# The first tile of rows loaded in two halves from two queues, and three issues reordered, in a two-layer attention and MLP kernel

## The chip, the cores and the metric

The kernel runs on one core of a Trainium2 chip. The metric is the device time of one execution in microseconds; lower is better. Times of single instructions come from one profiled execution.

## The reference

The input is a sequence of 2048 rows of 576 features in bfloat16. Four residual stages are applied, A, B, A, B:

```
x = x + A(layernorm(x));  x = x + B(layernorm(x));  and the same once more
A: q, k, v = x @ wqkv, 32 heads of 18
   phi(t) = where(t > 0, t + 1, exp(t)) + 1e-6
   kv = sum over rows of phi(k) v;  z = sum over rows of phi(k)
   o = phi(q) kv / (phi(q) z + 1e-6);  return o @ wo
B: y = layernorm(x);  h = gelu(y @ w1 + b1)   (576 -> 4608)
   return h @ w2 + b2                         (4608 -> 576)
```

## The kernel before

All weights and all rows stay in SBUF (on-chip memory). The rows are 16 tiles of 128 (`x_sb[:, t, :]`). For a tile, VectorE (DVE in the profile) computes the layer norm's statistics in two halves of 288 columns (`ln_st`, then `ln_mv`), GpSimd (POOL) the reciprocal standard deviation (`ln_rstd`), and VectorE the normalised rows (`y_ring`). TensorE (PE) transposes them into PSUM (`tp`), ScalarE (ACT) copies them to `yT`, and TensorE multiplies with the key and value weights `wkv_sb` into `k_ps`. ScalarE takes the exponential (`phi_e`), VectorE forms phi(k) (`pk`), and TensorE sums its products with the rows (`side_ps`, `rk_ps`).

Of the first weights, `wkv_sb`, there are five blocks of 128 input features; the fifth has 64 rows. A product for a half of the keys goes over the five blocks in order, so the last 64 rows are used last. `load_wkv(a, b, to)` asks for columns a to b: one DMA for the four whole blocks, one for the last 64 rows. The first half of the keys needs columns 0 to 288; the second product needs columns 288 to 576 and 72 value columns besides.

The order on every engine is written out by hand: each engine's wrapper (`vec`, `act`, `pool`, `sp`) chains every instruction to the one before it. DMAs are issued by SyncE (`sp`) or ScalarE (`act`) and stand in program order with that engine's other instructions; an instruction that waits for a semaphore holds all behind it on the same engine. In the trace the DMAs take eight completion semaphores in turn, and a DMA that reuses one is not issued before the earlier transfer with it has landed.

The kernel begins with lines 367 to 378: two tiles of rows and the first half of the key weights on SyncE, a dummy Exp on ScalarE (`act_dummy`, which brings the table of the exponential into ScalarE; it reads `neg_half`, written by GpSimd), the third tile on ScalarE, the second half of the key weights on SyncE, the 72 value columns on ScalarE, and three more tiles on SyncE. Meanwhile VectorE clears buffers, and TensorE runs ten products on zeros (`warm_ps`). Then come the first tile's statistics, `norms[0]`, the statistics of the second tile, the first tile's normalised rows in two pieces, its transposes, and so on: VectorE has the statistics of the first four tiles in front of the first `pk`.

Of the kernel before, what the change touches and what calls it, by code (L numbers as in the profile page):

```python
# [7 lines left out]
ACT = mybir.ActivationFunctionType  # L8
# [6 lines left out]
S, D, F, H, DH = 2048, 576, 4608, 32, 18  # L15
P = 128
# [14 lines left out]
HALF = D // 2  # L31
# [4 lines left out]
def build(tc, A_x, A_wqkv, A_wo, B_w1, B_b1, B_w2, B_b2, out, n_layers=4):  # L36
    nc = tc.nc
    with ExitStack() as ctx:
# [23 lines left out]
        vec, act = InOrder(nc.vector, "VectorE"), InOrder(nc.scalar, "ScalarE")  # L62
        pool, sp = InOrder(nc.gpsimd, "GpSimd"), InOrder(nc.sync, "SyncE")

        x_in = A_x.flatten_outer_dims()
# [32 lines left out]
        neg_half = const.tile([P, 1], F32, name="neg_half")  # L98
# [88 lines left out]
        wkv_sb = const.tile([P, KD, 2 * D], BF16, name="wkv_sb")  # L187
# [6 lines left out]
        x_sb = const.tile([P, NT, D], BF16, name="x_sb")  # L194
# [21 lines left out]
        act_dummy = const.tile([P, 1], F32, name="act_dummy")  # L216
# [104 lines left out]
        def load_x(t, by=sp):  # L321
            by.dma_start(out=x_sb[:, t, :], in_=x_in[t * P:(t + 1) * P, :])

        def load_wkv(a, b, to, by=sp):
            src, dst = slice(D + a, D + b), slice(to, to + b - a)
            by.dma_start(out=wkv_sb[:, 0:4, dst],
                         in_=A_wqkv[0:4 * P, src].rearrange("(k p) n -> p k n", p=P))
            by.dma_start(out=wkv_sb[0:64, 4, dst], in_=A_wqkv[4 * P:D, src])
# [36 lines left out]
            vec.tensor_copy(out=b1T[:], in_=tp[:, 0:NF])  # L365

        FIRST_X = 6
        load_x(0)
        load_x(1)
        load_wkv(0, HALF, 0)  # L370
        act.activation(out=act_dummy[:, 0:1], in_=neg_half[:, 0:1], func=ACT.Exp)
        load_x(2, act)
        load_wkv(HALF, D, HALF)
        load_wkv(D + V4, 2 * D, D, act)
        load_x(3)
        tc.add_manual_dep(sp.last_inst.ins, act.last, NOSYNC, reason="loads' order")
        load_x(4)
# [1071 lines left out]
@with_exitstack  # L1449
def kernel(  # L1450
    ctx: ExitStack,
    tc: tile.TileContext,
    A_x: bass.AP,
    A_wqkv: bass.AP,
    A_wo: bass.AP,
    B_x: bass.AP,
    B_w1: bass.AP,
    B_b1: bass.AP,
    B_w2: bass.AP,
    B_b2: bass.AP,  # L1460
    out: bass.AP,
):
    build(tc, A_x, A_wqkv, A_wo, B_w1, B_b1, B_w2, B_b2, out)
# [30 lines left out]
```

## Time and profile before

| what | value |
|---|---|
| median of 3 runs | 740.86 us (740.81 to 740.91) |
| profiled execution, time | 740.7 us |
| its span, first to last instruction | 738.8 us |
| TensorE busy | 733.3 us, 99% of the span |
| VectorE busy | 272.4 us, 37% |
| ScalarE busy | 300.8 us, 41% |
| granted TensorE clock | 1.0 throughout |
| DMA share, first 12.2 us | 0.76 |
| DMA share, after 60 us | 0.14 |

The share of an engine is busy time over the span; a wait on an engine costs time only where the chain that ends last goes through it. The time of an execution holds 1.9 us around the span. In rows of the timelines the first number is the start in microseconds from the span's start, the second the duration; an engine's name with a "q" is its sequencer, which issues DMAs; "x2" joins two instructions. Behind the row, in brackets, stands the idle time before it and what ended it.

### The profile page before, as it was taken

What the parts mean: (1) busy time and instruction counts of PE and PEld (TensorE: products, weight loads), DVE (VectorE), ACT (ScalarE), POOL (GpSimd) and SP (SyncE); (2) the same over time, 40 slices, a digit from 0 to 9 for tenths busy, and PEclk for the clock granted to TensorE, in tenths of its full rate; (3) what the DMA queues carried; (4) which work ended last, traced back from release to release, by engine and by line L of the source; (5) the groups of instructions that cost most, each with busy time, mean ns of one, the idle gap of its engine ahead of it and who ended that gap; (6) DMA issues with size and microseconds to landing.
All of it is one profiled execution on the core that took longest, in us unless ns stands there. A gap on an engine that the chain in (4) does not pass through costs nothing.

```text
span 738.8 us, 21166 instructions
## 1 busy us (share of the span) xinstructions
PE 733.3 (99%) x9142; PEld 578.4 (78%) x9151; DVE 272.4 (37%) x693; ACT 300.8 (41%) x667; POOL 131.9 (18%) x414
## 2 busy tenths in 40 slices
PE   8999999999999999999999999999999999999998
PEld 4666758996798679768987676789768976996695
DVE  8868744534224403300376594551410060000000
ACT  5776733007601740374035666220373047106700
POOL 4541000422121202200223120031300130010010
PEclk9999999999999999999999999999999999999999
DMA  8955220112200220110023001202020002000000
GB/s 203 245 172 182 76 76 29 26 31 52 36 11 26 37 38 18 31 24 2 18 77 94 24 6 31 74 2 55 17 37 2 18 19 35 10 18 10 1 18 17
DMA packets 61315, 35.02 MB, mean 47 GB/s; under 512 B 37126, under 2 KB 61222, under 8 KB 61222
## 3 DMA queue, kind: packets, MB, share of 16 engines
q1 hardware_dynamic: 60390, 33.43, 17.8%
q8 instruction: 71, 1.16, 0.7%
q10 hardware_dynamic: 832, 0.25, 0.2%
q14 instruction: 22, 0.18, 0.1%
HBM read 21.70 MB, written 4.93 MB: 36 GB/s over the span
## 4 chain that ended last, share of the span: by engine, by line
PE 98%; DVE 1%; DMA 0%; issue 0%; POOL 0%; DVEq 0%
PE m_ps L227 38%; PE hp_ps L227 20%; PE h_ps L227 18%; PE k_ps L227 5%; PE q_ps L227 5%; PE wo_ps L227 5%; PE rk_ps L227 4%; PE side_ps L227 1%; PE tp L476 0%; DVE ln_st L53 0%; PE den_ps L227 0%; PE kvwo_ps L227 0%; PE kv_ps L227 0%; DMA x_sb<-in_A_x_dram 0%; PE rden_ps L227 0%; DVE pk L53 0%
## 5 line engine op out<-in xcount | busy, mean ns | idle before, releaser
L227 PEld LDWEIGHTS <-units 64*128 64x128 bf16 (+1 forms) x5070 | 320.5, 94 | 12.9 <-issue 0.2
L227 PE MATMUL m_ps<-w_sb,units 64*128 64x288 bf16 (+2 forms) x4432 | 284.0, 283 | 0.0
L227 PEld LDWEIGHTS <-w_sb 64*128 64x128 bf16 x2304 | 163.8, 94 | 89.5 <-DVE rden L53 0.7
L227 PE MATMUL h_ps<-yT,w_sb 64*128 64x512 bf16 x1152 | 170.7, 376 | 0.0
L227 PE MATMUL hp_ps<-yT,w_sb 64*128 64x512 bf16 x1152 | 154.8, 376 | 0.0
L53 DVE TENSOR_TENSOR x_sb<-m_ps,xo 128x288 bf16<-128x288 f32 (+3 forms) x48 | 25.4, 554 | 335.9 <-PE m_ps L227 335.9
L53 ACT COPY relay_sb<-relay_sb 128x1 f32<-128x1 f32 x142 | 27.2, 191 | 261.6 <-PE m_ps L227 176.6
L53 ACT ACTIVATE units<-hp_ps,b1T 128x512 bf16<-128x512 f32 x144 | 91.2, 684 | 85.9 <-PE hp_ps L227 77.5
L53 POOL TENSOR_TENSOR xo<-x_sb,b_bc 128x576 f32<-128x576 bf16 x32 | 40.8, 1275 | 344.2 <-DVE x_sb L53 319.6
L53 ACT ACTIVATE units<-h_ps,b1T 128x512 bf16<-128x512 f32 x142 | 95.0, 688 | 0.2
L227 PE MATMUL k_ps<-wkv_sb,yT 64*128 64x288 bf16 (+3 forms) x432 | 60.2, 298 | 0.2 <-ACT yT L53 0.2
L227 PE MATMUL hp_ps<-yT,w_tail 64*128 64x512 bf16 x144 | 54.1, 376 | 0.0
L227 PE MATMUL h_ps<-yT,w_tail 64*128 64x512 bf16 x144 | 54.1, 376 | 0.0
L53 DVE BATCH_NORM_STATS2 ln_st<-x_sb 128x6 f32<-128x288 bf16 x128 | 51.6, 443 | 1.3 <-DMA x_sb<-in_A_x_dram 0.7
L227 PEld LDWEIGHTS <-yT 64*128 64x128 bf16 (+1 forms) x448 | 36.5, 95 | 8.4 <-ACT yT L53 0.5
L53 DVE STREAM_TRANSPOSE shared<-y_ring 128x640 bf16<-128x640 bf16 x40 | 32.7, 833 | 26.8 <-DMA yT<-shared 20.7
L227 PE MATMUL q_ps<-yT,wq_sb 64*128 64x512 bf16 (+2 forms) x273 | 41.6, 347 | 0.5
L53 POOL TENSOR_TENSOR ln_rstd<-ln_u,neg_half 128x1 f32<-128x1 f32 x64 | 36.5, 571 | 8.3 <-DVE ln_u L53 3.2
L53 ACT ACTIVATE phi_e<-k_ps 128x288 bf16<-128x288 f32 x64 | 26.3, 413 | 28.7 <-PE k_ps L227 28.3
L227 PE MATMUL wo_ps<-shared,units 64*128 64x288 bf16 (+1 forms) x480 | 38.0, 283 | 0.0
L53 DVE TENSOR_SCALAR y_ring<-x_sb,ln_mv,ln_rstd 128x576 bf16<-128x576 bf16 (+2 forms) x62 | 29.1, 476 | 23.8 <-POOL ln_rstd L53 23.0
L53 POOL MEMSET pool_relay<- 128x1 f32 x165 | 17.0, 103 | 114.8 <-PE hp_ps L227 43.9
(112 smaller groups left out, 493.3 us busy)
## 6 DMA issues: line engine op xcount, KB each, us to landing
yT<-shared SPq DMA_DIRECT2D x160, 40.0 KB
w_sb<-in_B_w_dram SPq DMA_DIRECT2D x12, 432.0 KB
w_sb<-in_B_w_dram SPq DMA_DIRECT2D x9, 512.0 KB
yT<-rden_rows SPq DMA_DIRECT2D x24, 126.0 KB
y_rows<-y_ring SPq DMA_DIRECT2D x16, 144.0 KB
units<-y_rows SPq DMA_DIRECT2D x16, 144.0 KB
x_sb<-in_A_x_dram SPq DMA_DIRECT2D x15, 144.0 KB
out_dram<-x_sb SPq DMA_DIRECT2D x15, 144.0 KB
```

Source lines behind the costliest of these rows:

```text
L53: inst = issue(*args, **kw)
L227: return pe(nc.tensor.matmul(out_, lhsT=lhsT, rhs=rhs, start=start, stop=stop, **kw))
```

## The change

The first tile of rows is asked for by two DMAs in place of one: columns 0 to 288 on SyncE, where the whole tile stood, and columns 288 to 576 on ScalarE. The last 64 rows of the first key weights (columns 0 to 288) move from SyncE, behind the four whole blocks, to the very front of ScalarE. The dummy Exp on ScalarE moves from ahead of ScalarE's DMAs to behind them all. The third tile's DMA stays on ScalarE, behind the two new ones. Nothing else differs; the whole of the data is the same, in one DMA more.

```diff
         FIRST_X = 6
-        load_x(0)
+
+        sp.dma_start(out=x_sb[:, 0, 0:HALF], in_=x_in[0:P, 0:HALF])
+        act.dma_start(out=wkv_sb[0:64, 4, 0:HALF], in_=A_wqkv[4 * P:D, D:D + HALF])
+        act.dma_start(out=x_sb[:, 0, HALF:D], in_=x_in[0:P, HALF:D])
         load_x(1)
-        load_wkv(0, HALF, 0)
-        act.activation(out=act_dummy[:, 0:1], in_=neg_half[:, 0:1], func=ACT.Exp)
+        sp.dma_start(out=wkv_sb[:, 0:4, 0:HALF], in_=A_wqkv[0:4 * P, D:D + HALF].rearrange("(k p) n -> p k n", p=P))
         load_x(2, act)
         load_wkv(HALF, D, HALF)
         load_wkv(D + V4, 2 * D, D, act)
+        act.activation(out=act_dummy[:, 0:1], in_=neg_half[:, 0:1], func=ACT.Exp)
         load_x(3)
         tc.add_manual_dep(sp.last_inst.ins, act.last, NOSYNC, reason="loads' order")
         load_x(4)
```

## The prediction

> **What bounds the kernel now.** First the page, part 4: which engine the end hangs on.
>
> ```profile
> PE 98%; DVE 1%; DMA 0%; issue 0%; POOL 0%; DVEq 0%
> ```
>
> TensorE carries 98% of the span, in an order that the change doesn't touch. So the change can only move the moment from which TensorE is never starved. For that moment I asked for the chain of waits of the first 13 us (start, us, what):
>
> ```profile
> 0.79 2.28 DMA x_sb<-in_A_x_dram
> 3.07 0.02 issue
> 3.09 0.83 DVE ln_st L53 x2
> ...
> 3.95 0.22 DVE ln_mv L53
> ...
> 4.34 0.73 DVE ln_st L53 x2
> 5.07 0.57 DVE y_ring L53 x2
> ...
> 12.19 0.92 PE k_ps L227 x5
> ```
>
> The first tile of rows lands at 3.07 (2.28 us after its issue), VectorE starts its statistics at 3.09, and from there the chain stays with VectorE (once GpSimd, 0.56 us of rstd) until TensorE takes over at 12.19. No piece between 3.09 and 12.19 waits for a transfer, so a shift of the end of the first tile's statistics (3.91) goes through to 12.19, and, as the chain is TensorE's from there, to the end of the kernel. That is the whole lever: before 3.09 there are 0.74 us of VectorE idle on a DMA.
>
> Next the queues that the change reorders, by the timelines of ScalarE and SyncE (start, us; "q" is the sequencer):
>
> ```profile
> 0.78 1.28 ACT L53 ACT_TABLE_LOAD   x1 [0.78 <-PEq L1478]
> 1.47 0.40 ACTq L53 DMA_DIRECT2D x_sb<-in_A_x_dram  x1
> 1.90 0.45 ACTq L53 DMA_DIRECT2D wkv_sb<-in_A_wqkv_dram  x1
> 2.08 0.20 ACT L53 ACTIVATE act_dummy<-neg_half 128x1 f32<-128x1 f32 x1
> 3.09 0.53 ACTq L53 DMA_DIRECT2D wkv_sb<-in_A_wqkv_dram  x1
> 5.83 0.75 ACT L53 COPY yT<-tp 128x384 bf16<-128x384 bf16 x2 [3.55 <-PE tp L476]
> ```
> ```profile
> 0.79 0.40 SPq L53 DMA_DIRECT2D x_sb<-in_A_x_dram  x1
> ```
> ```profile
> 0.79 0.87 SPq L53 DMA_DIRECT2D x_sb<-in_A_x_dram  x2
> 1.70 2.25 SPq L53 DMA_DIRECT2D wkv_sb<-in_A_wqkv_dram  x4
> 4.00 2.62 SPq L53 DMA_DIRECT2D x_sb<-in_A_x_dram  x3
> ```
>
> ScalarE's first DMA goes out at 1.47, while the table load still runs: it was held by the dummy ACTIVATE's semaphore (GpSimd's memset of neg_half ends at 1.43), not by the table. The third DMA, at 3.09, waited for the first tile's semaphore, 3.07: the trace shows eight DMA semaphores in turn, and each DMA waits for the eighth one before it.
>
> Call the loads X0, X1, X2 (tiles of rows), K0 and T0 (first key half: four blocks, last 64 rows), K1 and T1 (second half), V and VT. Last semaphore events in the trace: X0 3.07, X1 3.56, X2 4.56, K0 5.57, V 6.16, T0 6.27, K1 7.21, VT 7.39, T1 7.58, X3 7.79. The packet records run gap-free on most engines from 1.81, and in the order of issue. When they are wanted: X2 at 5.86, K0 and T0 at 6.37, K1, V, VT, T1 at 7.38 and after, X3 at 7.81.
>
> **Part 1: X0 in halves.** Half A alone on SyncE still starts at 0.79; its 128 packets of 576 bytes take 29 ns each in the records (K0's) against 51 ns of 1152 bytes: 8 packets an engine, 8 x 22 = 0.18 us less. Lone stores at the end of the trace agree: 1152 bytes a row land 1.76 us after issue, 256 bytes 1.49, so 576 bytes save 0.17. Half A: 3.07 - 0.18 = 2.89. Half B decides, because both halves' statistics (0.41 us each) must be over: today the second starts at 3.50 and ends at 3.91. A gain needs half B by 3.31 (2.89 + 0.02 + 0.41, then the second half follows at once).
>
> When does half B come? ScalarE's queue is free at 0.78, but T0 is in front, a load of 64 rows. Such issues are longer than 128-row ones: alone on an idle queue 0.53 us (370.24) against 0.33 to 0.34 (154.04):
>
> ```profile
> 370.24 0.53 SPq L53 DMA_DIRECT2D units<-wkv_sb  x1
> ...
> 154.04 0.34 SPq L53 DMA_DIRECT2D y_rows<-y_ring  x1
> ```
>
> So half B is issued at 0.79 + 0.53 + 0.04 = 1.36. SyncE issues X1 at 1.24 as now (0.40 + 0.05 after the first). X1 is 0.12 us earlier, so it is ahead on the 16 engines. Evidence: today X2 (ScalarE, 1.47) follows X1 (SyncE, 1.24); its first packet starts at 2.88, just after the first engine has finished X1 (2.83), and no engine took it earlier, though some finished X0 only at 2.67. Then half B lands after X0A + T0 + X1 + X0B where today X0 + X1 land at 3.56. Added: T0, 4 packets x 29 ns = 0.12; sixteen halves for eight wholes, 16 x 29 - 8 x 51 = 0.06. Half B: 3.56 + 0.18 = 3.74. The second statistics start at about 3.75 instead of 3.50: **+0.25 us**. Bounds: loads of 576 bytes show their semaphores 0.65 to 0.8 us after the last packet, X1 and X2 0.3 to 0.4, so up to +0.6; the other way, half B in front of X1 lands at 3.07 + 0.12 + 0.06 = 3.25, and the second half ends 0.41 + 0.41 after 2.91, at 3.74: -0.17. I take +0.25, from the nearest row (X1 behind X0).
>
> [...] The row: on each engine whole loads follow one another in the order of issue. [...]
>
> **Part 2: T0 in front, on ScalarE.** T0 lands with half B instead of at 6.27. It is the fifth product of k_ps, wanted at about 6.95; it wasn't late, so no gain. Its price is the 0.53 us in front of half B, counted above. On SyncE one issue of 0.60 us goes away: K1 is issued at 2.2 instead of 2.82. But the engines are busy anyway, and what must land before K1, T1, VT and X3 is the same number of bytes. Gain nothing, and it would fall on K1 to T1, for which the chain doesn't wait.
>
> X2 moves behind half B on ScalarE (issued 1.75, now 1.47) and so behind K0 (1.70). Worst case, strictly behind it: K0's 5.57 plus Part 1's 0.18 gives 5.75; wanted at 5.86 + 0.25. Cost 0, covered by 0.36 us (0.11 if the first tile isn't late). X3 ends in the same place, 7.8; wanted at 8.06. Cost 0; a gain in Part 1 beyond 0.02 us would meet it.
>
> **Part 3: the dummy Exp and its table behind the issues.** What stands ahead of the ACTIVATE now are five DMAs on ScalarE: T0, half B, X2, V, VT. The ninth and tenth DMA wait for the first and second semaphore (2.9 to 3.7). If VT is issued at 3.0 to 3.7 and takes 0.53, the table load runs until 4.8 to 5.6, the dummy 0.2 more: 5.0 to 5.8. Queued behind it is the first copy into yT (5.83 now, 6.08 with the late half): hidden, by 0.3 to 1.1 us. GpSimd's memset no longer holds a DMA: that is what lets T0 go at 0.79 instead of 1.47.
>
> **Sum.** Span 738.8 + 0.25 = 739.05; with the 1.9 us around it (execution 740.7) 740.95. The median of the runs, 740.86, lies 0.16 above that execution: **741.1**.
>
> **Rivals.** [...] (2) Slower beyond the measurable: VT gets the semaphore of K0 or X2 instead of X0A or T0, is issued at about 5.6, and the table load stands behind it: 5.6 + 0.53 + 1.28 + 0.2 = 7.6, and the yT copy wanted at 6.1 waits 1.5 us. TensorE's gaps before 12.19 give back 0.1 to 0.5 of it, so 1.0 to 1.4 beside Part 1's 0.25: about 742.3. It decides as soon as VT is issued later than 6.1 - 2.0 = 4.1. Against: K0 is the fifth DMA by issue time, so VT would have to be the thirteenth, and it is the tenth. (3) The load isn't changed in effect: half B and X1 share the engines so that half B lands near 3.5; 740.9.
>
> **Chances.** Forecast 0.63 (its own range 740.95 to 741.5), rival 1 0.22, rival 2 0.05, rival 3 0.10. The range 740.6 to 741.5 holds the forecast, rivals 1 and 3, and leaves out rival 2 and the far end of the late half. Measurable is 0.2%, 1.48 us. Only rival 2 at its worst with a late half reaches that: slower 0.04. Faster by that much isn't there to be had: even rows that landed before the memsets end (2.35) would bring 0.74 us; 0.01. Within: 0.95.
>
> **What would show it.** In the changed profile: ScalarE's first DMA at 0.79 and its second near 1.36; the first ln_st at 2.9, a gap of about 0.4 us ahead of the second, which starts at 3.7; TensorE's row at 12.19 near 12.45; the table load between 3.5 and 5.6 with no wait for ScalarE at the first yT copy. [...] All is wrong if the row at 12.19 doesn't follow the statistics' end.

## The result, and the profile after

| kernel | median, us | executions |
|---|---|---|
| before | 740.81 (740.60 to 741.14) | 13 |
| changed | 742.30 (741.92 to 743.60) | 13 |

The ratio is 1.0023, with a 95% interval of 1.0014 to 1.0032. The kernel became slower by 1.5 us where +0.25 was forecast, and the whole interval of the difference, 1.0 to 2.4 us, lies above the forecast. A second comparison gave the same: 742.12 against 740.85, 1.0021 [1.0013, 1.0030]. The profiled execution took 742.82 us, with a span of 741.1 against 738.8. Behind the changed lines the line numbers are 3 higher (L479 was L476). One execution of e1 (4438.87 us, the one that was profiled) and one of e15 (1573.06 us) lie far outside all others and move no median below by more than 0.03 us.

ScalarE first, in the changed kernel's timeline (start, duration, row; in brackets the idle time ahead of it and what ended it):

```profile
0.79 0.56 ACTq L53 DMA_DIRECT2D wkv_sb<-in_A_wqkv_dram  x1
1.38 1.07 ACTq L53 DMA_DIRECT2D x_sb<-in_A_x_dram  x2
2.49 1.02 ACTq L53 DMA_DIRECT2D wkv_sb<-in_A_wqkv_dram  x2
3.54 1.28 ACT L53 ACT_TABLE_LOAD   x1 [3.54 <-DMA wkv_sb<-in_A_wqkv_dram]
4.84 0.20 ACT L53 ACTIVATE act_dummy<-neg_half 128x1 f32<-128x1 f32 x1
6.79 0.75 ACT L53 COPY yT<-tp 128x384 bf16<-128x384 bf16 x2 [1.75 <-PE tp L479]
```

This is as forecast: T0 at 0.79, half B behind it at 1.38, the table load at 3.54. The dummy Exp ends at 5.04, and ScalarE then waits 1.75 us for TensorE's transposes, so the table is hidden.

VectorE, same view:

```profile
2.73 0.46 DVE L53 BATCH_NORM_STATS2 ln_st<-x_sb 128x6 f32<-128x288 bf16 x1 [0.38 <-DMA x_sb<-in_A_x_dram]
4.26 0.46 DVE L53 BATCH_NORM_STATS2 ln_st<-x_sb 128x6 f32<-128x288 bf16 x1 [1.07 <-DMA x_sb<-in_A_x_dram]
4.75 0.21 DVE L53 BATCH_NORM_AGGREGATE ln_mv<-ln_st 128x2 f32<-128x12 f32 x1
```

Half A is early (2.73; before, 3.09). Half B's semaphore comes at 4.23, the second statistics stand idle for 1.07 us, and `ln_mv` starts at 4.75, where it started at 3.95: +0.80.

TensorE before, then after:

```profile
5.46 0.53 PE L476 MATMUL tp<-ident,y_ring 128*128 128x128 bf16 x5 [0.44 <-DVE y_ring L53]
6.37 0.79 PE L227 MATMUL k_ps<-wkv_sb,yT 128*128 128x288 bf16 x5 [0.17 <-ACT yT L53]
```
```profile
6.26 0.71 PE L479 MATMUL tp<-ident,y_ring 128*128 128x128 bf16 x5 [0.93 <-DVE y_ring L53]
7.33 1.38 PE L227 MATMUL k_ps<-wkv_sb,yT 128*128 128x288 bf16 x5
```

The transposes start 0.80 us late, as the tile does. But now the same five products of `k_ps` take 1.38 us instead of 0.79: from the second on, one takes 448 ns instead of 286, and the next starts 0.24 us later instead of 0.12. That is half rate, and it lasts until about 9.7 us (before: until 4.6). So the row that stood at 12.19 stands at 13.77: +1.58, twice what the tile is late. The granted clock of the page is 1.000 throughout and doesn't show this; only the durations do.

From 12.19 to 387 us the distance stays 1.57 to 1.59. Then it grows once more, to 2.26 at 400 us, in the key sums of the second attention layer. The waits of 386 to 398 us in the changed kernel (engine and line, what it waits for: us in total, times, longest) hold one row that the kernel before has not:

```profile
PEld L227 <- POOL pool_relay L53: 1.2, 4, 0.4
```

`pool_relay` is a GpSimd memset that does nothing but pass a semaphore on: by the kernel's own order two streams of products on different rows of the array take turns on a PSUM bank, and the later one waits for it, 1.2 us in four waits by the row above. GpSimd of the kernel before at that place (in its second trace, e12), then GpSimd and VectorE of the changed kernel:

```profile
386.50 0.99 POOL L53 MEMSET pool_relay<- 128x1 f32 x5 [0.81 <-PE rk_ps L227]
```

```profile
389.06 0.26 POOL L53 MEMSET pool_relay<- 128x1 f32 x2 [0.42 <-PE k_ps L227]
```
```profile
388.78 0.28 DVE L53 TENSOR_SCALAR y_ring<-y_ring 128x512 bf16<-128x512 bf16 x1
```

The memset was released at 388.69 and starts at 389.06, when VectorE's instruction has ended; before, it ran 8 ns ahead of the same VectorE instruction, 85 ns after its release. That is 0.29 us. Three later memsets (391.34, 393.74 and 396.15) start 0.09 us into a VectorE instruction on `units` and take 0.23 us instead of 0.10, 0.13 us each: 0.68 in all.

So the trace of after has three terms: a half that lands late, products that run slow until 9.7 us, and late memsets. The experiments take them apart.

### The profile page after: what moved, and what is told of

Read it like the earlier page. It is cut to its first block, busy times and chain, and to the rows that moved or that the text cites. A ratio compares the mean times of both kernels' runs of the same rounds, so it can differ in the third digit from the quotient of the medians.

```text
span 741.1 us, 21168 instructions
## 1 busy us (share of the span) xinstructions
PE 735.4 (99%) x9142; PEld 579.3 (78%) x9151; DVE 272.5 (37%) x693; ACT 300.5 (41%) x667; POOL 131.6 (18%) x414
## 4 chain that ended last, share of the span: by engine, by line
PE 97%; DMA 1%; SPq 1%; ACTq 0%; issue 0%; DVE 0%
PE m_ps L227 38%; PE hp_ps L227 20%; PE h_ps L227 18%; PE k_ps L227 5%; PE q_ps L227 5%; PE wo_ps L227 5%; PE rk_ps L227 4%; PE side_ps L227 1%; SPq L53 1%; DMA wkv_sb<-in_A_wqkv_dram 1%; PE tp L479 0%; PE den_ps L227 0%; PE kvwo_ps L227 0%; DMA x_sb<-in_A_x_dram 0%; PE kv_ps L227 0%; PE rden_ps L227 0%
## 5 line engine op out<-in xcount | busy, mean ns | idle before, releaser
L227 PE MATMUL k_ps<-wkv_sb,yT 64*128 64x288 bf16 (+3 forms) x432 | 61.9, 302 | 0.0
L53 ACT ACTIVATE units<-q_ps 128x512 bf16<-128x512 f32 x60 | 32.7, 605 | 11.7 <-PE q_ps L227 11.5
```

What stands on the lines that cost most here:

```text
L53: inst = issue(*args, **kw)
L227: return pe(nc.tensor.matmul(out_, lhsT=lhsT, rhs=rhs, start=start, stop=stop, **kw))
```

## The experiments

"ln_mv" is the start of the first tile's. "Front" is the start of the fourth `k_ps` row, the 12.19 of the chain. "Steps" is what the shift against the first trace of before grows by between 385 and 400 us. Ratios are to the kernel before on the same chip.

| kernel | median, us | ratio (95%) | ln_mv | front | steps |
|---|---|---|---|---|---|
| before; again (e12) | 740.81; 740.87 | 0.9999 (0.999 to 1.0008) | 3.95; 3.99 | 12.19; 12.39 | 0 |
| changed | 742.30 | 1.0023 (1.0014 to 1.0032) | 4.75 | 13.77 | 0.69 |
| changed again (e11) | 742.12 | 1.0021 (1.0013 to 1.003) | 4.97 | 13.70 | 0.68 |
| first tile whole (e1; e8) | 741.02; 740.83 | 1.0001 (0.9992 to 1.001); 1.0003 (0.9994 to 1.0012) | 3.88 | 12.36 | 0 |
| half B ahead of T0 (e2) | 741.86 | 1.0014 (1.0005 to 1.0022) | 3.78 | 12.79 | 0.69 |
| changed, more warm-up (e3) | 741.89 | 1.0013 (1.0005 to 1.0022) | 4.56 | 12.81 | 0.69 |
| before, less warm-up (e4) | 741.91 | 1.0012 (1.0003 to 1.0021) | 3.91 | 13.40 | 0 |
| before, two halves on SyncE (e5) | 741.97 | 1.0017 (1.0009 to 1.0026) | 3.70 | 12.52 | 0.70 |
| before, table behind (e6) | 741.28 | 1.0008 (0.9999 to 1.0017) | 4.58 | 12.79 | 0 |
| half B first, T0 behind X2 (e7) | 741.57 | 1.0008 (1.0 to 1.0017) | 3.89 | 12.68 | 0.69 |
| before + 1 small DMA (e9) | 741.14 | 1.0003 (0.9993 to 1.0012) | 3.93 | 12.53 | 0 |
| changed + 7 small DMAs (e10) | 741.32 | 1.0008 (1.0 to 1.0017) | 4.61 | 12.82 | 0 |
| changed + VectorE op (e13) | 742.70 | 1.0022 (1.0013 to 1.0031) | 4.68 | 13.60 | 0.72 |
| the same, more warm-up (e14) | 741.88 | 1.0014 (1.0005 to 1.0023) | 4.59 | 12.93 | 0.72 |
| before + VectorE op (e15) | 740.92 | 1.0001 (0.9992 to 1.001) | 3.91 | 12.60 | 0 |
| changed + 1 small DMA (e16) | 741.31 | 1.0008 (0.9998 to 1.0017) | 4.72 | 13.95 | 0 |
| before, X5 in halves (e17) | 740.85 | 1.0001 (0.9991 to 1.001) | 4.01 | 12.36 | 0 |
| two halves + 7 small DMAs (e18) | 741.26 | 1.0008 (0.9998 to 1.0017) | 3.76 | 12.50 | 0 |

### Which part of the change: the whole tile, and half B ahead

First tile whole on SyncE, T0 and the table as in the change:

```diff
-        sp.dma_start(out=x_sb[:, 0, 0:HALF], in_=x_in[0:P, 0:HALF])
+        load_x(0)
         act.dma_start(out=wkv_sb[0:64, 4, 0:HALF], in_=A_wqkv[4 * P:D, D:D + HALF])
-        act.dma_start(out=x_sb[:, 0, HALF:D], in_=x_in[0:P, HALF:D])
```

> The first tile whole again on SyncE; the 64 rows in front on ScalarE and the dummy Exp behind the issues stay. Theory 'late half and clock' (half B lands 1.2 us later than the whole tile did, the statistics end 0.8 us later, TensorE idles over 0.9 us and runs its next products at half rate until about 9.8): the tile lands near 3.1, the products run at full rate from 5.5, the first k_ps row of the third tile is back at 12.2 and the time at 740.8, within 0.2. Rival 'weights late' (the new order delays V, VT and the second half of the key weights, and that costs the time): their order is as in the changed kernel, so at least half of the 1.5 us stays, 741.5 or more.

Half B ahead of T0 on ScalarE:

```diff
+        act.dma_start(out=x_sb[:, 0, HALF:D], in_=x_in[0:P, HALF:D])
         act.dma_start(out=wkv_sb[0:64, 4, 0:HALF], in_=A_wqkv[4 * P:D, D:D + HALF])
-        act.dma_start(out=x_sb[:, 0, HALF:D], in_=x_in[0:P, HALF:D])
```

> The changed kernel with half B in front of the 64 rows on ScalarE. Theory 'late half and clock': half B is issued at 0.79, lands near 2.9, the statistics end near 3.6 instead of 3.9, TensorE stays at full rate; X3, which landed at 8.0 in the changed kernel, is wanted at 7.5 and caps the gain: 740.5 to 740.9. Rival 'weights late': 742, as V, VT and the second half of the key weights are where they are in the changed kernel.

The whole tile gave 741.02, the time of before. The same kernel was run again for its trace:

> The changed kernel with the first tile whole on SyncE: the same kernel as the run with the whole tile, for its trace. Theory: X0 lands at 3.0 to 3.1, the statistics end within 0.1 us of before, the nine products ahead of the transposes reach full rate as before (the k_ps products near 286 ns), TensorE's front moves by less than 0.2 us, and the time is 741.0 as in the first run of it. Rival (T0 in front and the table behind the issues move the end through late weights): the tile is on time and k_ps waits for wkv, with a front 0.3 us or more late.

740.83, again the time of before: X0 lands at 3.01, `ln_mv` starts at 3.88. The front is 0.17 late (12.36), as the first two groups of products wait 0.28 and 0.18 us for weights. So T0 in front and the table behind the issues together cost nothing that the times show (ratios 1.0001 and 1.0003); the loss comes with the halves.

With half B ahead, the halves gave what they promise: `ln_mv` starts at 3.78, 0.17 earlier than before, and TensorE's transposes at 5.29. But it isn't kept: 741.86, where 740.5 to 740.9 was expected. VectorE and TensorE of that run:

```profile
6.21 0.46 DVE L53 BATCH_NORM_STATS2 ln_st<-x_sb 128x6 f32<-128x288 bf16 x1 [0.43 <-DMA x_sb<-in_A_x_dram]
```
```profile
7.87 1.55 PE L227 MATMUL k_ps<-wkv_sb,yT 128*128 128x360 bf16 x10 [0.36 <-DMA wkv_sb<-in_A_wqkv_dram]
```

X2, the third load on ScalarE, lands at 6.19 and the tile that needs it waits 0.43 us; then the second group of products waits 0.36 us for weights. The front is at 12.79. An early first tile meets late second loads: the rival "weights late" is right here, while in the changed kernel the tile is later than the weights, and no row waits for them.

### Products that run slow

The changed kernel with three more products on zeros:

```diff
-NWARM = 10
+NWARM = 13
```

> The changed kernel with 13 products on zeros instead of 10: TensorE is busy until 5.6 to 6.4 while the half is late. Theory 'late half and clock': the first tile is as late as in the changed kernel (+0.8 us), but its products run at full rate, 0.12 us apart instead of 0.24, and the loss falls from 1.5 to about 0.8 us: 741.6, with the row of the third tile's k_ps near 13.0 instead of 13.8. Rival 'weights late': the products on zeros change nothing, 742.3.

The kernel before with three fewer (`NWARM = 7`):

> The kernel before with 7 products on zeros instead of 10, its loads untouched: the clock by itself. TensorE is idle from about 4.2 to 5.5. Theory 'late half and clock': the first tile's products run at half rate, the row of the third tile's k_ps moves from 12.2 to 12.5 to 13.1, time 741.1 to 741.7. Rival 'weights late', under which the pause of TensorE plays no part: 740.8, no change.

TensorE of the first, then of the second:

```profile
6.40 0.52 PE L479 MATMUL tp<-ident,y_ring 128*128 128x128 bf16 x5
7.38 0.79 PE L227 MATMUL k_ps<-wkv_sb,yT 128*128 128x288 bf16 x5 [0.24 <-ACT yT L53]
```
```profile
5.68 0.72 PE L476 MATMUL tp<-ident,y_ring 128*128 128x128 bf16 x5 [1.64 <-DVE y_ring L53]
6.90 1.36 PE L227 MATMUL k_ps<-wkv_sb,yT 128*128 128x288 bf16 x5
```

With twelve products ahead of the transposes there is no idle time, and `k_ps` is at full rate (0.79) although half B is as late as ever (`ln_mv` 4.56); the front shifts by 0.62, the tile's delay of 0.61. With six, the kernel before idles 1.64 us and gets the slow products (1.36) with its tile on time; front and time, 13.40 and 741.91, are beyond the 12.5 to 13.1 and the 741.1 to 741.7 that were expected. The 741.89 of e3 is 0.3 above its 741.6. So the slow products belong to the idle time ahead of the transposes.

It doesn't happen in every execution. The times of the changed kernel lie in two groups. In its three samples (changed, e11, e13; 35 executions) 19 are at 741.69 to 742.30 and 16 at 742.61 to 743.60, about 0.9 us apart; of the slowest, 743.28 to 743.60, no trace was taken. All three profiled executions (742.82, 742.76, 742.70) are of the upper group and have the slow products. That the others of that group have them too is inferred from the times. With `NWARM = 13` there is one group: 22 executions of e3 and e14, 741.69 to 742.29. The changed kernel with seven small DMAs (e10, below) was profiled in its lower group, and its `k_ps` took 0.79 in spite of 0.79 us of idle time. For before such times are rare (742.15, 742.29 and 742.46, one in each of three samples of 33).

The products pass to full rate once, at a moment that differs: at about 4.1 us (e15), 4.2 (e5, e6), 4.6 (before), 5.7 (e12), 6.5 (e3), 7.0 (e9); and at 9.4 to 10.2 in after, e11, e13, e16 and e4. In these traces products start at 1.31, and the passage comes 2.8 to 5.7 us later where TensorE is kept busy until then (e12 idles 0.17 us). In the five that have it at 9.4 to 10.2 a gap of 0.9 to 1.6 us lies ahead of it (0.93 in after, 1.64 in e4); with the shorter gap of e10, 0.79, `k_ps` was at full rate. Behind the passage gaps of 1.13 and 1.28 us (e15, e6) brought no slow products (`k_ps` 0.79 in e6, front 12.60 in e15). Why a gap ahead of it should put the passage off is not shown; that filling the gap takes the slow products away is (`k_ps` 0.79 in e3 and e14).

### Halves alone, table alone, and another order

```diff
-        load_x(0)
+        for a in (0, HALF):
+            sp.dma_start(out=x_sb[:, 0, a:a + HALF], in_=x_in[0:P, a:a + HALF])
```

> The kernel before, with the first tile asked for as two halves, both from SyncE, and nothing else: T0, the exponential table and all the rest stay where they were. It has one DMA more, as the changed kernel has. Theory (late half and clock): half B is next in its own queue, ahead of X1, so it lands by about 3.3, the second statistics follow the first at once or within 0.1 us, and TensorE's front moves by -0.2 to +0.1 us; no slow products. Time within 0.3 us of before, if the 0.7 us at 387 us come from a shift of the front. Rival for those 0.7 us (one DMA more puts every later instruction of GpSimd and VectorE in another phase, whatever the front does): the front stays within 0.2 us of before and the end moves by +0.7 all the same, about 741.5. Rival for the front (halves as such are slow: two transfers of 576 bytes a row cost more than one of 1152): the second statistics start 0.3 to 0.8 us late as in the changed kernel, 741.6 to 742.

The halves as such are not late: `ln_mv` starts at 3.70, 0.25 earlier than before. The front is +0.33 all the same, as X1 behind them lands at 4.44 (before: 3.56) and the first products wait 0.37 us for weights. And the steps at 387 us are there, in a kernel that differs from before in nothing but this one load.

```diff
-        act.activation(out=act_dummy[:, 0:1], in_=neg_half[:, 0:1], func=ACT.Exp)
         load_x(2, act)
         load_wkv(HALF, D, HALF)
         load_wkv(D + V4, 2 * D, D, act)
+        act.activation(out=act_dummy[:, 0:1], in_=neg_half[:, 0:1], func=ACT.Exp)
```

> The kernel before, with only the dummy Exp behind ScalarE's issues; the first tile is whole and T0 in its old place. Theory: ScalarE's first DMA, X2, goes out at about 0.8 instead of 1.47, and so ahead of X1 (1.24) on the engines; X1 lands about 0.5 us later (3.56 to about 4.1; wanted at 4.34), X0 stays at about 3.0 to 3.1, the table load ends before the yT copy at 5.8. TensorE's front moves by less than 0.1 us and the time is that of before within 0.3 us. Rival (the table behind the issues has a price of its own, through a late V or VT issue or a late yT copy): the first yT copy waits for ScalarE, and the time is 0.3 us or more above before.

A miss: 741.28, with the front at 12.79. The table is hidden, but X2 goes out at 0.79, in the same moment as X0 on the other queue: X0 lands at 3.70 (before: 3.07), X2 at 3.88, and `ln_mv` starts 0.63 late. Without the dummy Exp ahead of it, ScalarE's first load goes out with the first tile (0.79, where it was 1.47); in the changed kernel that is T0, half the rows at half the bytes each, and e8 shows that it does no harm (`ln_mv` 3.88, ratio 1.0003).

Half B first on ScalarE, then X2, then T0, the table behind:

> Halves from two queues, with half B first on ScalarE (0.79), X2 behind it and T0 only behind X2; the dummy Exp behind the issues. Theory (late half and clock; T0 in front has a price and no gain): both halves land at 2.8 to 3.0, the statistics run back to back from 2.9 and end 0.15 us earlier than before; X2 is issued at about 1.2 and lands well before 5.8, so the stall on X2 that the run with half B ahead of X1 had (0.43 us) is gone; TensorE's front moves by -0.2 to 0, limited by K0 and T0, wanted at 6.2. The time is 740.7 to 740.9 without the 0.7 us at 387 us, 741.4 to 741.6 with them. Rival (weights late: every byte that comes ahead of them costs TensorE its length, whatever the tile does): k_ps waits for wkv by 0.3 us or more, and the front is +0.3 or later in spite of the early tile, 741.2 or more.

`ln_mv` 3.89, X2 in time, but `k_ps` starts at 6.64 instead of 6.37, as K0 lands at 6.51, and its second group waits again for weights (0.16 us); 741.57, of which the steps are 0.69. The best so far of the kernels with halves from two queues (e10 and e16 below, without steps, come to 741.3), and none is faster than before.

### The steps at 387 us

Up to here they came with every kernel that has the first tile in halves, and with none else. Those have one DMA more, and the DMAs take eight semaphores in turn (in before ScalarE's third, issued at 3.09, has X0's semaphore, which came at 3.07). A small DMA, of 8 rows by 16 bytes, was added behind all tiles of rows:

```diff
         for t in range(FIRST_X, NT):
             load_x(t)
+        for i in range(1):
+            sp.dma_start(out=pad_sb[:, i, :], in_=x_in[0:8, 8 * i:8 * (i + 1)])
```

> The kernel before with one more DMA on SyncE, of 8 rows by 16 bytes into a tile that nothing reads, issued behind all the tiles of rows (after 10 us); nothing of the first loads is touched. It asks where the 0.7 us at 387 us come from. Theory (one DMA more moves every later DMA to the next of eight semaphores, and with it the race of GpSimd's relay memset against VectorE's y_ring at 387 us): front within 0.1 us of before, then +0.2 us steps between 387 and 395 us, 0.65 to 0.7 in all; about 741.5. Rival (they come from the two halves, or from how late the front is): no step at 387 us, the time is that of before, 740.9.

The same seven times (`range(7)`) in the changed kernel:

> The changed kernel with seven more such small DMAs behind the tiles of rows, so that it has eight more than the kernel before and each later DMA has the semaphore that it had there. Theory (semaphores in turn): the front stays late by 0.8 to 1.6 us as in the changed kernel, and the steps at 387 to 395 us are gone: 0.7 us less than the changed kernel, 741.6. Rival (any DMA more brings them, or the halves do): they stay, 742.3 or above.

Both kernels once more beside them:

> The changed kernel itself once more, for how far the two terms of its front repeat. Theory (late half and clock): half B lands at 4.0 to 4.3, the products of k_ps ahead of 8 us take 380 to 450 ns in place of 286, TensorE's front is 1.2 to 1.7 us late, and the 0.7 us at 387 us are there; 742.3. Rival (the slow products were one run's chance): the products are at full rate, the front is late by the tile's delay alone, and the time is near 741.9.

> The kernel before once more, for how far its first loads repeat. Theory: the first tile lands at 3.0 to 3.1, X1 at 3.5 to 3.7, TensorE's front within 0.15 us of the first trace, the time is that of before. Rival (the first loads differ by some tenths of a us from one execution to the next, so that the late half is within their spread): X1 lands 0.3 us or more away from 3.56, and the front moves by 0.3 us or more.

One DMA more in that place brings no steps to before (its front, at 12.53, is late because the products pass to full rate only at 7.0). Before itself repeats within 0.2 us: X0 lands at 3.11, X1 at 3.66, the front is at 12.39; so the late half is no spread of the loads. The changed kernel repeats its late half (`ln_mv` 4.97), its slow products and its steps. Seven small DMAs take the steps from the changed kernel, and the time falls from 742.12 to 741.32 on the same chip. The chain of the changed kernel's second trace is the clearest picture of its front (start, us, what):

```profile
1.38 3.07 DMA x_sb<-in_A_x_dram
...
4.48 0.47 DVE ln_st L53
...
4.97 0.22 DVE ln_mv L53
...
6.48 0.71 PE tp L479 x5
```

It goes from half B's issue through its landing at 4.46 to the transposes. (In the first trace the chain ran by a late wq load instead, which says less.)

Was it a race of a few ns between the memset and VectorE's y_ring, an instruction of `q_sum`? A VectorE memset of 128x1 was put ahead of that:

```diff
             def q_sum(dst, e):
+                vec.memset(pad_sb[:], 0.0)
                 vec.tensor_scalar(out=e, in0=e, scalar1=1.0, scalar2=1e-6, op0=ALU.min, op1=ALU.add)
```

> The changed kernel with one VectorE memset of 128x1 ahead of each of the two instructions of q_sum, of which y_ring at 387 us is one: VectorE comes some 60 ns later to that instruction and GpSimd's relay memset a like time earlier than it. Theory (the 0.7 us are a race of a few ns: the instruction that starts first holds the other, and TensorE waits for the memset): the memset runs ahead of y_ring, no step at 387 to 395 us, and the time is 0.6 to 0.7 us below the changed kernel, 741.4 to 741.6, still in two groups 0.9 us apart (clock). Rival (the steps have another cause, such as the semaphores of the later DMAs): they stay, 742.2.

> The same, and NWARM 13 for 10, so that TensorE is busy until the first tile's transposes: both late costs of the changed kernel are taken away and the late half is left alone. Theory: half B lands at 4.0 to 4.4 and TensorE's front is late by what the tile's statistics are late, 0.6 to 0.9 us; full rate from the first k_ps; no steps at 387 us; all executions in one group at 741.3 to 741.6. Rival (the three terms don't add, as waits for weights stand behind the late tile anyway): 741.9 or above.

> The kernel before with the same VectorE memset ahead of q_sum: the control for its own cost. Theory: VectorE isn't the bound there, and the kernel before has no steps at 387 us to lose: 740.8 to 741.0. Rival (the added instruction costs TensorE time, or brings the race about): 741.3 or above.

The steps stayed. The edit moved y_ring's start by 9 ns only, not by 60, so it is a weak test; but GpSimd's memset, due 85 ns after its release, would have started 17 ns ahead of y_ring and was held all the same, while 8 ns were enough in before. In nineteen traces (all but e1's) it was due 7 to 18 ns ahead of y_ring, in those where it was held as in those where it ran. The order of the recorded starts doesn't decide it. The control, 740.92, shows that the added instruction costs nothing. With 13 products (e14) the slow products are gone and the steps are not, so it repeats e3: 741.88 in one group, above the 741.3 to 741.6 that was expected without steps.

Last, the turn of semaphores against the halves against any small DMA:

```diff
-        for t in range(5, FIRST_X):
-            load_x(t)
+        for a in (0, HALF):
+            sp.dma_start(out=x_sb[:, 5, a:a + HALF], in_=x_in[5 * P:6 * P, a:a + HALF])
```

> The kernel before with the sixth tile of rows asked for as two halves on SyncE in place of one load: one DMA more, far behind the first statistics, and no other tile than those it had. Theory (turn of eight): the steps appear at 387 to 395 us, 741.4 to 741.6, with TensorE's front that of before. Rival (only the first tile in halves brings them): no steps, 740.8 to 741.0.

> The changed kernel with one small DMA (8 rows by 16 bytes, into a tile that nothing reads) behind the tiles of rows: two DMAs more than the kernel before, where the run without the steps had eight more. Theory (the steps at 387 us come with the place of the later DMAs in the turn of eight semaphores): they stay, as the turn is moved by two; 742.0 to 742.3. Rival (any small DMA behind the tiles takes them away): they are gone, 741.3 to 741.6.

> The first tile as two halves, both from SyncE, T0 and the table as before, and seven small DMAs behind the tiles: eight DMAs more than the kernel before. Theory (turn of eight): no steps, 0.7 us below the run of the two halves alone; 741.1 to 741.3. Rival (halves of the first tile bring the steps, and the run of the changed kernel without them was a chance): they stay, 741.8 to 742.1.

A tile in halves elsewhere brings no steps (740.85), and two or eight DMAs more have none (e16, e18). GpSimd in e16, changed but for one small DMA:

```profile
388.07 1.00 POOL L53 MEMSET pool_relay<- 128x1 f32 x5 [0.80 <-PE rk_ps L228]
```

Five memsets in a row, none held. The turn of semaphores falls: moved by one it has steps (e5) and has none (e9, e17). What is shown is the size (0.67 to 0.72 us, in all seven kernels with the first tile in halves and no small DMA) and the place (one memset held by 0.29 us behind y_ring, and three that take 0.23 us). Why exactly these seven have it stays open. The kernels with small DMAs also have the tile that these fill (8 rows of 128 bytes in on-chip memory); no run has that tile without the DMAs, so which of the two takes the steps away isn't shown.

What holds the memset isn't shown by any run. In the trace of after the first one starts at the end of y_ring, 388.78 + 0.28. But in e13 it started 18 ns ahead of the recorded end, and the three later memsets start, by the records, 0.09 us inside a VectorE instruction and last longer (0.23 us instead of 0.10).

## Why the prediction was wrong, point by point

**What bounds the kernel.** Right: TensorE from 12.19, and ahead of it the first tile's chain. Wrong: "a shift of the end of the first tile's statistics (3.91) goes through to 12.19, and [...] to the end". It goes through once with a factor (the slow products) and grows once more at 387 us. Both are terms that the sum doesn't have.

**Part 1, half B: the mechanism right, the size off.** The issue at 1.36 was 1.38, and half B did land behind X1, in all seven traces of the changed kernel's front. Forecast landing 3.74; measured 4.05 to 4.46. `ln_mv` starts at 4.56 to 4.97, 4.70 in the mean of the seven, against 3.97 in the two traces of before: +0.73 where the sum had +0.25. The step that failed is "4 packets x 29 ns" and "16 x 29 - 8 x 51": packets priced at their medians, 29 and 51 ns. The 192 packets of T0 and half B took 44 ns in the mean in the changed kernel's first trace (median 29), as nine of them took 0.11 to 0.86 us; in before, too, X0's 128 packets took 76 ns in the mean, against the 51 of the sum. Half B's last packet ended at 3.91 (3.70 to 4.12 in the seven traces), where X1's last in before, 3.27, and the sum's 0.18 give 3.45. ("8 x 22" erred the other way: half A landed at 2.60 to 2.70, not at 2.89, and gained nothing, as half B decides.) The row of the windows (start:end, busy time of the engines, clock, DMA share, GB/s) shows the same for all loads. Before, then after:

```profile
2.80:4.00 1.20, 1.20 (x4) 0.45 (x3) 0.87 (x3) 0.00 (x0) 0.76 (x2) 1.00 1.02 258
```
```profile
2.80:4.00 1.20, 1.20 (x4) 0.46 (x3) 0.39 (x1) 0.46 (x1) 0.75 (x2) 1.00 0.93 186
```

In 2.8 to 4.0 the engines are nearly as busy (0.93 against 1.02) and move 28% less. The text's bound of +0.6 rested on something else, semaphores 0.65 to 0.8 us behind the last packet; half B's came 0.32 to 0.37 behind it, and the +0.73 lies beyond the bound. Of the late statistics 0.3 to 0.5 us remain in the time: without steps the changed kernel has 741.31 and 741.32 against 740.82 and 740.85 (e16, e10), and e14 less its steps is 0.32 above before.

**Order on the engines (rivals 1 and 3).** In all seven traces X1 (issued at 1.24) and half B (1.37 to 1.39) landed in order of issue, at 3.96 and 4.23 in the changed kernel's first trace. Half B ahead of X1, with the -0.17 of Part 1 (rival 1 of the chances), is shown by none. Loads issued in the same moment landed 0.18 us apart (X0 and X2 in e6, 3.70 and 3.88). Rival 3, half B near 3.5 by sharing with X1, fell by half B's landings, 4.05 to 4.46.

**Part 2.** T0 without gain, and without price by itself: right (e8). "Cost 0" for X2: X2 landed at 5.96 in the changed kernel, not 5.75, and was covered by the late tile alone. As soon as the tile is early (e2) it costs 0.43, and the weights 0.36. The gain of -0.17 with half B in front wasn't to be had: e2 is at +0.9 us.

**Part 3.** Right in every number, at the early end: table load at 3.54 (3.5 to 5.6), dummy over at 5.04 (5.0 to 5.8), no wait at the yT copy. Rival 2 fell with it, though the time it gave, 742.3, is the one measured.

**The missing step: what TensorE does in the gap.** The forecast named the second `ln_st` but not the idle time that a late tile opens ahead of the transposes. The nine products on zeros end at 5.33 when they are slow throughout; the tile's delay makes the gap 0.79 to 1.15, and by the times in their two groups that costs 0.9 us more in 16 of 35 executions: this term stood at nothing. The steps at 387 us are the other term that the sum doesn't have; their cause stays open.

**The sum again.** Late half 0.45, steps 0.69, slow products 0.9 in 16 of 35, 0.41 in the mean: 1.55. The means of the three samples are 1.71, 1.48 and 1.66 above before.

**What would show it.** "All is wrong if the row at 12.19 doesn't follow the statistics' end": it didn't, 13.77 for a tile that is late by 0.80.

## What to carry to other kernels

In these runs splitting the first load over two queues brought the tile earlier only where both halves were first in their queues (`ln_mv` 3.78 in e2 and 3.89 in e7, against 3.95 and 3.99 in before), and even that won nothing, as the loads behind came later: X2 cost e2 0.43 us, the weights 0.36, and they cost e7's second group 0.16. With T0 in front of it half B landed at 4.05 to 4.46, and the second statistics waited for it (1.07 us in after). Where TensorE is kept busy ahead of its first real work, ask what a late tile does to that cover: three more products on zeros made the time here steady (741.69 to 742.29 in 22 executions of e3 and e14, against 741.69 to 743.60 in 35 of the changed kernel). And a change of one DMA at the start moved the time by 0.70 us some 380 us later (e5; 0.67 to 0.72 in all seven kernels that have the steps), so look for the place where the shift between two traces grows, and not at the front alone.

## What the runs showed of the hardware beyond that

- Loads issued together: two loads of a tile of rows from two queues, both at 0.79, land 0.18 us apart, and the first one 0.63 us later than where the second is issued at 1.47 (e6, before).
- TensorE passed to full rate anywhere between 4.1 (e15) and 10.2 us in these traces, while the granted clock in the profile reads 1.000.
- A GpSimd memset of 128x1 that takes 0.10 us started 0.37 us after its release (0.085 in before) where a VectorE instruction of 0.28 us ran, and took 0.23 us where it started 0.09 us into one (after).
